# Transposing attention inputs by the DMA crossbar instead of TensorE, in a fused attention and feed-forward kernel

## The chip, the cores and the metric

One core of one Trainium2 chip. The metric is the device time of one execution in microseconds (us). The profiler's span, used for everything inside an execution, is 1.7 to 2.7 us shorter than that execution's time. The "granted clock" is the share of its full clock that TensorE was allowed, as the trace records it.

## The reference, cut to what matters

```python
# x: 8 batches, 8 heads, 512 tokens, 64 wide; state: 8, 8, 32, 64
a      = softmax(x @ state.T / 8);   xread = a  @ state     # tokens read the state
a2     = softmax(state @ x.T / 8);   sread = a2 @ x         # the state reads the tokens
y      = concat(xread, sread)        # 544 rows of 512 per batch
h      = y @ w_in                    # 512 -> 2048
g      = h + sin(alpha * h)**2 / (alpha + 1e-9)
out    = g @ w_out                   # 2048 -> 512
```

Two transposed operands are wanted per batch: x, to form the scores, and the softmax weights, to use them as a moving operand.

## The kernel before: the parts that matter

The kernel works in nine blocks t of 16 steps f. Block t makes g for batch t (block 8 does the state reads of all batches), and prepares the attention of batch t + 1 between its steps.

```python
def pack(a, g, parts=2):             # VectorE: x from head-major to token-major order ("repack")
    nc.vector.tensor_copy(a.xp[:, :, hs, :], xnat_l[a.b][:, hs, :].rearrange("p h (i d) -> p i h d", i=C))

def T(a, g):                         # 8 TensorE transposes of x, then a copy out of PSUM
    ...  nc.tensor.transpose(tp[:, k, i*P:(i+1)*P], a.pair(i, 2*g + k), ident[:])
    nc.vector.tensor_copy(a.xT[:, 2*g:2*g+2, :], tp[:])

def AT_(a, gs):  ...                 # the same for the softmax weights

def mm1(t, f):                       # h: PSUM pool of four buffers
    hp = psH.tile(...); two matmuls
    nc.scalar.activation(s, hp, ACT.Sin, scale=alpha)
    nc.gpsimd.tensor_tensor(s2, s, s, ALU.mult)
def snake(t, f, ...):                # the combine; frees the h buffer; issued two steps later
    nc.vector.scalar_tensor_tensor(gT, s2, inva, hp, ALU.mult, ALU.add)

# slots of block t, n = batch t+1          (steps; post = after the step's other work)
#   T at 0, 1   scores S at 3, 4   Exp X post 4   W at 6, column sums Cs at 7
#   row sums Rs post 7, 8   normalise N post 8, 9   AT_ at 12   m_step at 9, 11, 13, 15
#   load of x(t+2) post 5,  repack of x(t+2) post 15
```

`Cs` ends in a 128x128 reciprocal and two products on VectorE. `m_step` multiplies state by a quarter ("slab") of w_in. In all traces here an engine runs its instructions in program order.

The softmax here doesn't subtract the row's maximum and nothing guards it: scores larger than these inputs give would overflow.

Of the kernel before, what the change touches and what calls it, by code (L numbers as in the profile page):

```python
# [12 lines left out]
BF16 = mybir.dt.bfloat16  # L13
FP32 = mybir.dt.float32
# [4 lines left out]
def kernel(  # L19
# [9 lines left out]
    nc = tc.nc  # L29
# [4 lines left out]
    C = S // P  # L34
# [11 lines left out]
    const = ctx.enter_context(tc.tile_pool(name="const", bufs=1))  # L46
    wpool = ctx.enter_context(tc.tile_pool(name="wpool", bufs=1))
    xpool = ctx.enter_context(tc.tile_pool(name="xpool", bufs=3))
    xppool = ctx.enter_context(tc.tile_pool(name="xppool", bufs=3))
    apool = ctx.enter_context(tc.tile_pool(name="apool", bufs=2))  # L50
    smallp = ctx.enter_context(tc.tile_pool(name="smallp", bufs=2))
    gpool = ctx.enter_context(tc.tile_pool(name="gpool", bufs=2))
    sinp = ctx.enter_context(tc.tile_pool(name="sinp", bufs=4))
    outp = ctx.enter_context(tc.tile_pool(name="outp", bufs=3))
# [29 lines left out]
    w_in_sb = wpool.tile([P, Q, DFF], BF16, name="w_in_sb")  # L84
    w_in_v = moe_w_in.rearrange("(q p) f -> p q f", p=P)
    for k in range(FS):
        nc.gpsimd.dma_start(
            w_in_sb[:, :, k * FW:(k + 1) * FW], w_in_v[:, :, k * FW:(k + 1) * FW]
        )
    load_x(1, 1)  # L90
    w_out_sb = wpool.tile([P, FT, DOUT], BF16, name="w_out_sb")
    w_out_v = moe_w_out.rearrange("(ft p) c -> p ft c", p=P)
    for k in range(4):
# [22 lines left out]

    def prep_state():
        st2 = const.tile([P, 16, 2, D], BF16, name="st2")
        nc.vector.tensor_copy(
            st2[:], st_nat[:].unsqueeze(2).to_broadcast([P, 16, 2, D])  # L120
        )
        for half in range(2):
            tp = psX.tile([P, 8, P], BF16, name="st_ps", tag="px")
            for k in range(8):
                nc.tensor.transpose(
                    tp[:, k, :],
                    st2[:, half * 8 + k].rearrange("p r d -> p (r d)"),
                    ident[:],
                )
            for r in range(2):  # L130
                rows = slice(r * D, (r + 1) * D)
                src = tp[rows].rearrange("d k (e r2 jh) -> d e r2 jh k", r2=2, jh=2)
                dst = stT[rows].rearrange(
                    "d bg (h2 r2 jh hf k) -> d (bg h2) r2 jh hf k", h2=2, r2=2, jh=2, hf=2
                )
                if r == 0:
                    nc.vector.tensor_copy(dst[:, :, r, :, half, :], src[:, :, r])
                else:
                    nc.scalar.copy(dst[:, :, r, :, half, :], src[:, :, r])


    class Att:
# [2 lines left out]
            a.xp = xppool.tile([P, C, H, D], BF16, name="xp")  # L145

        def alloc(a):
            a.xT = apool.tile([P, Q, S], BF16, name="xT")
            a.E = apool.tile([P, G, C, P], BF16, name="E")
            a.A = apool.tile([P, G, C, P], BF16, name="A")  # L150
            a.AT = apool.tile([P, G, S], BF16, name="AT")
            a.R = smallp.tile([P, G, C * HH], FP32, name="R")
            a.rR = smallp.tile([P, G, C * HH], FP32, name="rR")
            a.sp = {}
# [11 lines left out]
        def T(a, g):  # L166
            tp = psX.tile([P, 2, S], BF16, name="x_ps", tag="px")
            for k in range(2):
                for i in range(C):
                    nc.tensor.transpose(  # L170
                        tp[:, k, i * P:(i + 1) * P], a.pair(i, 2 * g + k), ident[:]
                    )
            nc.vector.tensor_copy(a.xT[:, 2 * g:2 * g + 2, :], tp[:])  # L173

        def S(a, g):
            sp = psX.tile([P, C, P], FP32, name="s_ps", tag="px")
            for i in range(C):
                for k in range(2):
                    cols = slice(k * 2 * Ns, (k + 1) * 2 * Ns)
                    nc.tensor.matmul(  # L180
                        sp[:, i, cols],
                        a.xT[:, 2 * g + k, i * P:(i + 1) * P],
                        stT[:, a.b * G + g, cols],
                        start=True, stop=True,
                    )
            a.sp[g] = sp
# [68 lines left out]
    def m_step(b, fs, on_act):  # L255
        if fs == 0:
            Ms[b] = apool.tile([P, G, DFF], BF16, name="M")
        mp = [psX.tile([P, FW], FP32, name="m_ps", tag="px") for _ in range(G)]
        for h in range(2):
            for g in range(G):  # L260
                for r in range(2):
# [40 lines left out]
            gT[t][:, f, :n], s2[:, :n], inva_sb[:, f:f + 1], hp[:, :n], ALU.mult, ALU.add  # L302
        )

    def mm2(t, st, f0, f1, box):
        if f0 == 0:
            box[0] = psO.tile([P, DOUT], FP32, name="o_ps")
        op = box[0]
        for ft in range(f0, f1):
            nc.tensor.matmul(  # L310
                op[:], gT[t][:, ft, st * P:(st + 1) * P], w_out_sb[:, ft, :],
# [2 lines left out]
        if f1 == FT:  # L314
            o_sb = outp.tile([P, DOUT], FP32, name="o_sb")
            nc.scalar.copy(o_sb[:], op[:])  # L316
            if t < B:
                r0 = t * TB + st
                nc.sync.dma_start(out[r0:r0 + C * (P - 1) + 1:C, :], o_sb[:])
            else:  # L320
                for k in range(P // Ns):
                    r0 = (st * (P // Ns) + k) * TB + S
                    nc.sync.dma_start(out[r0:r0 + Ns, :], o_sb[k * Ns:(k + 1) * Ns, :])

    atts, Ms, gT = {}, {}, {}


    warm_up(12)
# [17 lines left out]
        m_step(0, k, (True, True))  # L346
    a.AT_([0])
    a.AT_([1])
    for k in range(2, 4):
        m_step(0, k, (True, True))  # L350
    atts[1] = Att(1)
    atts[1].pack(0, 1)

    LAG = 2
    pend = []
    box = [None]
    for t in range(B + 1):
        gT[t] = gpool.tile([P, FT, S], BF16, name="gT")
        pe, post = {}, {}

        def add(d, s, fn, *args):
            d.setdefault(s, []).append((fn, args))

        if t + 1 < B:
            n = atts[t + 1]
            n.alloc()
            add(pe, 0, n.T, 0)
            add(pe, 1, n.T, 1)
            add(pe, 3, n.S, 0)
            add(pe, 4, n.S, 1)  # L370
            add(post, 4, n.X, 0)
            add(post, 4, n.X, 1)
            add(post, 7, n.Rs, 0)
            add(post, 8, n.N, 0, nc.gpsimd)
            add(post, 8, n.Rs, 1)
            add(post, 9, n.N, 1, nc.gpsimd)
            add(pe, 12, n.AT_, [0, 1])
            for k, s in enumerate((9, 11, 13, 15)):
                add(pe, s, m_step, t + 1, k, (True, t == 0))
        if t < B:  # L380
            s = 6 if t + 1 < B else 0
            add(pe, s, atts[t].W)
            add(pe, s + 1, atts[t].Cs)
        if t + 2 < B:
            def nxt(b=t + 2):
                atts[b] = Att(b)
                atts[b].pack(0, 1)
            add(post, 5, load_x, t + 2, 1)
            add(post, 15, nxt)
        for f in range(FT):  # L390
            cur = mm1(t, f)
            for fn, args in pe.get(f, []):
# [1 line left out]
            pend.append((t, f) + cur)  # L394
            if len(pend) > LAG:
                snake(*pend.pop(0))
            if t > 0:
                mm2(t - 1, f // 4, (f % 4) * 4, (f % 4) * 4 + 4, box)
            for fn, args in post.get(f, []):
                fn(*args)  # L400
    while pend:
        snake(*pend.pop(0))
    for st in range(B * Ns // P):
        for k in range(4):
            mm2(B, st, 4 * k, 4 * k + 4, box)
# [1 line left out]
_INS = ['x', 'state', 'moe_w_in', 'moe_w_out', 'moe_alpha']  # L407
_OUTS = [((4352, 512), 'float32')]
# [25 lines left out]
```

## Time and profile before

| | before |
|---|---|
| time, median (the profiled execution: 265.33) | 266.09 us |
| first Sin of block 0 | 21.18 us |
| block 0, first Sin to first Sin | 24.46 us |
| block 1 | 26.93 us |
| blocks 2 to 6 | 27.27, 27.26, 27.26, 27.26, 27.12 us |
| block 7 | 22.02 us |
| first Sin of block 8 to the end | 32.77 us |

The seams between blocks are taken at the Sin of step 0. Each block switches ScalarE to Exp and back, and for 3.4 us GpSimd gets no new Sin: the Exp gap. A timeline gives start, length, engine; in brackets the idle time ahead and what ended it.

```profile
107.78 1.28 ACT L189 ACT_TABLE_LOAD   x1
112.06 0.96 DVE L243 RECIPROCAL rC<-w_ps 128x128 f32<-128x128 f32 x1 [2.39 <-PE w_ps L236]
112.24 1.04 POOL L297 TENSOR_TENSOR s<-s 128x512 bf16<-128x512 bf16 x1 [3.36 <-ACT s L295]
113.67 0.75 DVE L301 SCALAR_TENSOR_TENSOR gT<-s,inva_sb,h_ps 128x512 bf16<-128x512 bf16 x1
114.47 0.59 PE L284 MATMUL h_ps<-AT,M 128*128 128x512 bf16 x2 [0.21 <-DVE gT L301]
```

The reader is to see the order: VectorE starts the reciprocal at 112.06, before GpSimd has its first square after the gap, so most of that work lies in time that VectorE would have idled away. TensorE then waits only 0.21 us for an h buffer.

### The profile page before, as it was taken

The numbers are of one execution on the slowest core, as the hardware profiler recorded it, in microseconds if no ns is written. First come the engines' busy times: TensorE is split into PE (matmuls) and PEld (weight loads), VectorE is DVE, ScalarE is ACT, GpSimd is POOL, SyncE is SP. The second block draws the span as 40 slices with busy tenths as digits, with TensorE's granted clock in tenths as the row PEclk, the third lists the DMA queues.
The fourth block names the chain that finished last, engine by engine and source line by source line (L and its number), as shares of the span: only waits on it lengthen the run. The fifth ranks groups of instructions, "written<-read, shape, count | busy, mean of one in ns | idle before, by whom it ended". The sixth has DMA issues, their size and how long they took to land.

```text
span 263.5 us, 4423 instructions
## 1 busy us (share of the span) xinstructions
PE 231.6 (88%) x1630; PEld 110.2 (42%) x1660; DVE 164.2 (62%) x267; ACT 160.0 (61%) x254; POOL 171.8 (65%) x183
## 2 busy tenths in 40 slices
PE   6667557998989898989899989998999999999991
PEld 2424213543455344534453445434444444456640
DVE  3733667749774978397758866687668685543310
ACT  2454968495649664966487557865685655644420
POOL 8713599749844985499548955696659668854400
PEclk9856968999999999999999999999999999999997
DMA  7999860018111711172115411361111111111112
GB/s 84 201 201 205 148 80 4 1 41 120 42 42 40 115 47 40 40 110 53 40 42 82 78 44 41 56 105 40 42 41 40 42 40 40 42 55 64 44 62 59
DMA packets 19782, 17.86 MB, mean 68 GB/s; under 512 B 2992, under 2 KB 15280, under 8 KB 19760
## 3 DMA queue, kind: packets, MB, share of 16 engines
q0 software_dynamic: 12704, 8.65, 23.4%
q1 hardware_dynamic: 7056, 8.92, 10.3%
q8 instruction: 13, 0.21, 0.3%
q14 instruction: 9, 0.07, 0.1%
HBM read 17.31 MB, written 8.91 MB: 100 GB/s over the span
## 4 chain that ended last, share of the span: by engine, by line
PE 63%; DVE 21%; DMA 5%; POOL 4%; issue 3%; ACT 1%; ACTq 0%; POOLq 0%
PE o_ps L310 35%; PE h_ps L284 15%; DVE gT L301 8%; DMA xnat<-in_x_dram 5%; PE x_ps L170 3%; DVE R L193 3%; DVE rC L243 3%; PE h_ps L290 3%; DVE M L276 3%; PE m_ps L265 2%; POOL s L297 2%; DVE xp L158 2%; DVE xs_all L246 2%; PE w_ps L225 2%; DVE rR L194 1%
## 5 line engine op out<-in xcount | busy, mean ns | idle before, releaser
L297 POOL TENSOR_TENSOR s<-s 128x512 bf16<-128x512 bf16 (+1 forms) x144 | 141.7, 995 | 77.0 <-ACT s L295 76.8
L295 ACT ACTIVATE s<-h_ps,alpha_sb 128x512 bf16<-128x512 f32 (+1 forms) x144 | 94.0, 666 | 75.8 <-PE h_ps L284 63.7
L310 PE MATMUL o_ps<-w_out_sb,gT 128*128 128x512 bf16 x523 | 135.7, 380 | 2.0 <-issue 1.0
L301 DVE SCALAR_TENSOR_TENSOR gT<-s,inva_sb,h_ps 128x512 bf16<-128x512 bf16 (+1 forms) x144 | 99.9, 712 | 34.1 <-POOL s L297 33.9
L284 PE MATMUL h_ps<-AT,M 128*128 128x512 bf16 x247 | 76.5, 390 | 9.7 <-DVE gT L301 9.3
L310 PEld LDWEIGHTS <-gT 128*128 128x128 bf16 x544 | 48.6, 98 | 50.9 <-issue 5.5
L284 PEld LDWEIGHTS <-M 128*128 128x128 bf16 x256 | 24.9, 99 | 41.4 <-issue 15.9
L316 ACT COPY o_sb<-o_ps 128x512 f32<-128x512 f32 x34 | 20.0, 588 | 10.7 <-PE o_ps L310 9.2
L274 ACT CAST M<-m_ps 128x512 bf16<-128x512 f32 x40 | 22.4, 583 | 3.2 <-PE m_ps L265 3.2
L276 DVE CAST M<-m_ps 128x512 bf16<-128x512 f32 x24 | 16.2, 676 | 10.8 <-PE m_ps L265 10.8
L243 DVE RECIPROCAL rC<-w_ps 128x128 f32<-128x128 f32 x8 | 7.7, 957 | 17.0 <-PE w_ps L236 17.0
L265 PE MATMUL m_ps<-w_in_sb,stT 64*32 64x512 bf16 x256 | 16.3, 422 | 2.2 <-ACT M L274 2.0
L170 PE MATMUL x_ps<-ident,xp 128*128 128x128 bf16 x128 | 10.5, 231 | 7.5 <-DVE xp L158 7.5
L173 DVE COPY xT<-x_ps 128x1024 bf16<-128x1024 bf16 x16 | 11.0, 691 | 9.2 <-PE x_ps L170 9.2
L170 PEld LDWEIGHTS <-xp 128*128 128x128 bf16 x128 | 8.5, 104 | 13.5 <-DVE xp L158 11.5
L265 PEld LDWEIGHTS <-stT 64*32 64x32 bf16 x256 | 4.3, 90 | 17.6 <-issue 15.1
L193 DVE TENSOR_REDUCE R<-E 128x16 f32<-128x512 bf16 x16 | 10.8, 676 | 0.5 <-ACT E L189 0.5
L189 ACT ACTIVATE E<-s_ps 128x512 bf16<-128x512 f32 x16 | 8.8, 595 | 1.8 <-PE s_ps L180 1.6
L290 PE MATMUL h_ps<-xs_all,w_in_sb 128*128 128x256 bf16 x64 | 9.6, 273 | 0.1
L219 DVE COPY AT<-a_ps 128x1024 bf16<-128x1024 bf16 (+1 forms) x9 | 5.7, 632 | 6.1 <-PE a_ps L216 6.0
L189 ACT ACT_TABLE_LOAD x7 | 9.0, 1283 | 0.1
L295 ACT ACT_TABLE_LOAD x7 | 9.0, 1283 | 0.1
(41 smaller groups left out, 107.5 us busy)
## 6 DMA issues: line engine op xcount, KB each, us to landing
out_dram<-o_sb SPq DMA_DIRECT2D x32, 256.0 KB, 2.2
xnat<-in_x_dram POOLq DMA_DIRECT2D x7, 512.0 KB, 8.2
w_in_sb<-in_moe_w_in_dram POOLq DMA_DIRECT2D x4, 512.0 KB, 9.9
w_out_sb<-in_moe_w_out_dram POOLq DMA_DIRECT2D x4, 512.0 KB, 19.5
xnat<-in_x_dram POOLq DMA_DIRECT2D x2, 256.0 KB, 5.7
out_dram<-o_sb SPq DMA_DIRECT2D x8, 64.0 KB, 1.7
st_nat<-in_state_dram POOLq DMA_DIRECT2D x1, 256.0 KB, 4.8
alpha_sb<-in_moe_alpha_dram SPq DMA_DIRECT2D x1, 8.0 KB, 3.0
```

The lines of the kernel that those rows point to most:

```text
L170: nc.tensor.transpose(tp[:, k, i * P:(i + 1) * P], a.pair(i, 2 * g + k), ident[:])
L189: nc.scalar.activation(a.E[:, g], a.sp[g][:], ACT.Exp, scale=scale)
L193: nc.vector.reduce_sum(a.R[:, g], E8, axis=AX.X)
L265: nc.tensor.matmul(mp[g][o0:o0 + Ns, :], stT[rows, b * G + g, c0:c0 + Ns], w_in_sb[rows, 2 * g + h, fs * FW:(fs + 1) * FW], start=True, st ...
L274: nc.scalar.copy(dst, mp[g][:])
L276: nc.vector.tensor_copy(dst, mp[g][:])
L284: nc.tensor.matmul(hp[:, :n], Ms[t][:, g, f * P:(f + 1) * P], atts[t].AT[:, g, :], start=(g == 0), stop=(g == G - 1),)
L295: nc.scalar.activation(s[:, :n], hp[:, :n], ACT.Sin, scale=alpha_sb[:, f:f + 1])
L297: nc.gpsimd.tensor_tensor(s2[:, :n], s[:, :n], s[:, :n], ALU.mult)
L301: nc.vector.scalar_tensor_tensor(gT[t][:, f, :n], s2[:, :n], inva_sb[:, f:f + 1], hp[:, :n], ALU.mult, ALU.add)
L310: nc.tensor.matmul(op[:], gT[t][:, ft, st * P:(st + 1) * P], w_out_sb[:, ft, :], start=(ft == 0), stop=(ft == FT - 1),)
L316: nc.scalar.copy(o_sb[:], op[:])
```

## The change

Its intent: take 24 transposes per batch, and the copies out of PSUM, off TensorE and VectorE for batches 1 to 7; start block 0 as soon as half of w_in is there; spread block 0's output matmuls over blocks 0 and 1; shorten the end. The core of the diff (smaller edits at the head, which engine evicts what above all, are left out):

```diff
     for k in range(FS):
+        if k == 2:
+            load_x(1, 1)
         nc.gpsimd.dma_start(w_in_sb[...k], w_in_v[...k])
-    load_x(1, 1)
...
+        def T_dma(a):
+            nc.sync.dma_start_transpose(a.xT..., a.xp...)
+        def AT_dma(a):
+            nc.sync.dma_start_transpose(a.AT..., a.A...)
...
+        if t == 0:    # block 0: batch 1 packed and transposed after step 0, w_in slabs 2, 3 at steps 4, 6
+            add(post, 0, att, 1, "T_dma")
+            ss, xs, rs, tr = (2, 3), 3, 8, 11;   ps = (14, 15);   ms = steps 8, 10, 12, 14
+        else:
+            ss, xs, rs, tr = (1, 2), 2, 5, 8;    ps = (12, 13)
+            ws = [(5, 6, t)] ...                # W and Cs;  W and Cs of batch 0 in block 1
+        # S at ss, X post xs, Rs post rs, rs+1, N one later, AT_dma post tr
+        # load of x(t+2) post 3, repack post ps[0], ps[1], T_dma post ps[1]
...
+        if t == 0:  two[f] = two tiles of block 0's output matmuls, 2 + 2 per step, from step 9 on
...                  # the rest of them in block 1; later blocks as before
+            # last stores: one DMA per row tile, by a 3-d view
+            ov = out.rearrange("(b t) c -> b t c", t=TB)
+            eng.dma_start(ov[st * n:(st + 1) * n, S:, cols], o_sb[:, cols])
+    # and the last tile in two halves of 256 columns, evicted by ScalarE and VectorE
```

The pools for xp, the attention tiles and the small tiles get one more buffer.

More of the change, by code (lines that the diff above doesn't have):

```diff
@@ L48 @@
     xpool = ctx.enter_context(tc.tile_pool(name="xpool", bufs=3))
-    xppool = ctx.enter_context(tc.tile_pool(name="xppool", bufs=3))
-    apool = ctx.enter_context(tc.tile_pool(name="apool", bufs=2))
-    smallp = ctx.enter_context(tc.tile_pool(name="smallp", bufs=2))
+    xppool = ctx.enter_context(tc.tile_pool(name="xppool", bufs=4))
+    apool = ctx.enter_context(tc.tile_pool(name="apool", bufs=3))
+    epool = ctx.enter_context(tc.tile_pool(name="epool", bufs=3))
+    smallp = ctx.enter_context(tc.tile_pool(name="smallp", bufs=3))
     gpool = ctx.enter_context(tc.tile_pool(name="gpool", bufs=2))
@@ L118, in prep_state @@
         st2 = const.tile([P, 16, 2, D], BF16, name="st2")
-        nc.vector.tensor_copy(
-            st2[:], st_nat[:].unsqueeze(2).to_broadcast([P, 16, 2, D])
-        )
+        for half in range(2):
+            js = slice(half * 8, (half + 1) * 8)
+            nc.vector.tensor_copy(
+                st2[:, js], st_nat[:, js].unsqueeze(2).to_broadcast([P, 8, 2, D])
+            )
         for half in range(2):
@@ L135, in prep_state @@
                 )
-                if r == 0:
-                    nc.vector.tensor_copy(dst[:, :, r, :, half, :], src[:, :, r])
-                else:
-                    nc.scalar.copy(dst[:, :, r, :, half, :], src[:, :, r])
+                nc.scalar.copy(dst[:, :, r, :, half, :], src[:, :, r])
     class Att:
@@ L147, in alloc @@
         def alloc(a):
-            a.xT = apool.tile([P, Q, S], BF16, name="xT")
-            a.E = apool.tile([P, G, C, P], BF16, name="E")
+            a.xT = apool.tile([P, C, Q, P], BF16, name="xT")
+            a.E = epool.tile([P, G, C, P], BF16, name="E")
             a.A = apool.tile([P, G, C, P], BF16, name="A")
@@ L172, in T @@
                     )
-            nc.vector.tensor_copy(a.xT[:, 2 * g:2 * g + 2, :], tp[:])
+            nc.vector.tensor_copy(
+                a.xT[:, :, 2 * g:2 * g + 2, :],
+                tp[:].rearrange("p k (i t) -> p i k t", i=C),
+            )
+        def T_dma(a):
+            nc.sync.dma_start_transpose(
+                a.xT[:].rearrange("p i q t -> p (i q) t"),
+                a.xp[:].rearrange("p i h d -> p (i h d)"),
+            )
+        def AT_dma(a):
+            nc.sync.dma_start_transpose(
+                a.AT[:].rearrange("p g (i t) -> p (g i) t", i=C),
+                a.A[:].rearrange("p g i c -> p (g i c)"),
+            )
         def S(a, g):
@@ L181, in S @@
                         sp[:, i, cols],
-                        a.xT[:, 2 * g + k, i * P:(i + 1) * P],
+                        a.xT[:, i, 2 * g + k, :],
                         stT[:, a.b * G + g, cols],
@@ L257, in m_step @@
             Ms[b] = apool.tile([P, G, DFF], BF16, name="M")
-        mp = [psX.tile([P, FW], FP32, name="m_ps", tag="px") for _ in range(G)]
+        if b == 0 and fs < 2:
+            mp = [psH.tile([P, FW], FP32, name="h_ps") for _ in range(G)]
+        else:
+            mp = [psX.tile([P, FW], FP32, name="m_ps", tag="px") for _ in range(G)]
         for h in range(2):
@@ L303, in snake, with mm2 @@
         )
-    def mm2(t, st, f0, f1, box):
+    def mm2(t, st, f0, f1):
         if f0 == 0:
-            box[0] = psO.tile([P, DOUT], FP32, name="o_ps")
-        op = box[0]
+            ops[t, st] = psO.tile([P, DOUT], FP32, name="o_ps")
+        op = ops[t, st]
         for ft in range(f0, f1):
@@ L316, in mm2, with store, mm2_last @@
             nc.scalar.copy(o_sb[:], op[:])
-            if t < B:
-                r0 = t * TB + st
-                nc.sync.dma_start(out[r0:r0 + C * (P - 1) + 1:C, :], o_sb[:])
-            else:
-                for k in range(P // Ns):
-                    r0 = (st * (P // Ns) + k) * TB + S
-                    nc.sync.dma_start(out[r0:r0 + Ns, :], o_sb[k * Ns:(k + 1) * Ns, :])
-    atts, Ms, gT = {}, {}, {}
+            store(t, st, o_sb, slice(0, DOUT), nc.sync)
+    def store(t, st, o_sb, cols, eng):
+        if t < B:
+            r0 = t * TB + st
+            eng.dma_start(out[r0:r0 + C * (P - 1) + 1:C, cols], o_sb[:, cols])
+        else:
+            n = P // Ns
+            ov = out.rearrange("(b t) c -> b t c", t=TB)
+            eng.dma_start(ov[st * n:(st + 1) * n, S:, cols], o_sb[:, cols])
+    def mm2_last(t, st):
+        o_sb = outp.tile([P, DOUT], FP32, name="o_sb")
+        for k in range(2):
+            op = psO.tile([P, DOUT], FP32, name="o_ps")
+            cols = slice(k * DOUT // 2, (k + 1) * DOUT // 2)
+            for ft in range(FT):
+                nc.tensor.matmul(
+                    op[:, cols], gT[t][:, ft, st * P:(st + 1) * P], w_out_sb[:, ft, cols],
+                    start=(ft == 0), stop=(ft == FT - 1),
+                )
+            if k == 0:
+                nc.scalar.copy(o_sb[:, cols], op[:, cols])
+                store(t, st, o_sb, cols, nc.sync)
+            else:
+                nc.vector.tensor_copy(o_sb[:, cols], op[:, cols])
+                store(t, st, o_sb, cols, nc.scalar)
+    atts, Ms, gT, ops = {}, {}, {}, {}
     warm_up(12)
@@ L348, with plan @@
     a.AT_([1])
-    for k in range(2, 4):
-        m_step(0, k, (True, True))
-    atts[1] = Att(1)
-    atts[1].pack(0, 1)
-    LAG = 2
-    pend = []
-    box = [None]
-    for t in range(B + 1):
-        gT[t] = gpool.tile([P, FT, S], BF16, name="gT")
+    def plan(t):
         pe, post = {}, {}
@@ L362, in add @@
             d.setdefault(s, []).append((fn, args))
-        if t + 1 < B:
-            n = atts[t + 1]
-            n.alloc()
-            add(pe, 0, n.T, 0)
-            add(pe, 1, n.T, 1)
-            add(pe, 3, n.S, 0)
-            add(pe, 4, n.S, 1)
-            add(post, 4, n.X, 0)
-            add(post, 4, n.X, 1)
-            add(post, 7, n.Rs, 0)
-            add(post, 8, n.N, 0, nc.gpsimd)
-            add(post, 8, n.Rs, 1)
-            add(post, 9, n.N, 1, nc.gpsimd)
-            add(pe, 12, n.AT_, [0, 1])
-            for k, s in enumerate((9, 11, 13, 15)):
-                add(pe, s, m_step, t + 1, k, (True, t == 0))
@@ L380, with nxt, att @@
-        if t < B:
-            s = 6 if t + 1 < B else 0
-            add(pe, s, atts[t].W)
-            add(pe, s + 1, atts[t].Cs)
-        if t + 2 < B:
-            def nxt(b=t + 2):
-                atts[b] = Att(b)
-                atts[b].pack(0, 1)
-            add(post, 5, load_x, t + 2, 1)
-            add(post, 15, nxt)
+        def nxt(b, k):
+            if k == 0:
+                atts[b] = Att(b)
+            atts[b].pack(k)
+        def att(b, m, *args):
+            getattr(atts[b], m)(*args)
@@ new lines, in plan @@
+        n = t + 1
+        if t == 0:
+            for k in range(2):
+                add(post, 0, nxt, 1, k)
+            add(post, 0, att, 1, "alloc")
+            add(post, 0, att, 1, "T_dma")
+            add(pe, 4, m_step, 0, 2, (True, False))
+            add(pe, 6, m_step, 0, 3, (True, False))
+            ss, xs, rs, tr = (2, 3), 3, 8, 11
+            ms, ws = ((8, True, True), (10, True, False), (12, True, False), (14, True, False)), []
+            ps = (14, 15)
+        else:
+            ss, xs, rs, tr = (1, 2), 2, 5, 8
+            ms = ((8, True, False), (10, True, False), (12, True, False), (14, True, False))
+            ws = [(5, 6, t)] if n < B else [(0, 1, t)][:B - t]
+            if t == 1:
+                ws.append((11, 11, 0))
+            ps = (12, 13)
@@ new lines, in plan @@
+        if n < B:
+            for g in range(G):
+                add(pe, ss[g], att, n, "S", g)
+                add(post, xs, att, n, "X", g)
+                add(post, rs + g, att, n, "Rs", g)
+                add(post, rs + 1 + g, att, n, "N", g, nc.gpsimd)
+            add(post, tr, att, n, "AT_dma")
+            for k, (s, *on) in enumerate(ms):
+                add(pe, s, m_step, n, k, on)
+        for s0, s1, b in ws:
+            add(pe, s0, att, b, "W")
+            add(pe, s1, att, b, "Cs")
@@ new lines, in plan @@
+        if t + 2 < B:
+            add(post, 3, load_x, t + 2, 1)
+            for k in range(2):
+                add(post, ps[k], nxt, t + 2, k)
+            add(post, ps[1], att, t + 2, "alloc")
+            add(post, ps[1], att, t + 2, "T_dma")
+        two = {}
+        if t == 0:
+            for f in range(9, FT):
+                two[f] = [(0, st, 2 * (f - 9), 2 * (f - 8)) for st in range(2)]
+        elif t == 1:
+            two[1] = [(0, 0, 14, 16), (0, 1, 14, 16)]
+            for f in range(2, FT):
+                k0, k1 = 32 * (f - 2) // 14, 32 * (f - 1) // 14
+                for h in range(2):
+                    a0, a1 = max(k0, 16 * h), min(k1, 16 * h + 16)
+                    if a0 < a1:
+                        two.setdefault(f, []).append((0, 2 + h, a0 - 16 * h, a1 - 16 * h))
+        else:
+            for f in range(FT):
+                two[f] = [(t - 1, f // 4, (f % 4) * 4, (f % 4) * 4 + 4)]
@@ L390 @@
+        return pe, two, post
+    LAG = 2
+    pend = []
+    for t in range(B + 1):
+        gT[t] = gpool.tile([P, FT, S], BF16, name="gT")
+        pe, two, post = plan(t)
         for f in range(FT):
@@ L396 @@
                 snake(*pend.pop(0))
-            if t > 0:
-                mm2(t - 1, f // 4, (f % 4) * 4, (f % 4) * 4 + 4, box)
+            for args in two.get(f, []):
+                mm2(*args)
             for fn, args in post.get(f, []):
@@ L402 @@
         snake(*pend.pop(0))
-    for st in range(B * Ns // P):
-        for k in range(4):
-            mm2(B, st, 4 * k, 4 * k + 4, box)
+    n = B * Ns // P
+    for st in range(n - 1):
+        mm2(B, st, 0, FT)
+    mm2_last(B, n - 1)
 _INS = ['x', 'state', 'moe_w_in', 'moe_w_out', 'moe_alpha']
```

## The prediction

> **What bounds the kernel now.** I read the page's busy rows first, then busy time in stretches, then TensorE's waits, then the timeline of one block. The program runs nine blocks, t = 0 to 8, of 16 steps. A step is two matmuls into h_ps (L284), Sin on ScalarE, a square on GpSimd, a combine on VectorE (L301), and four output matmuls (L310) for the block before. The attention of the next block is slotted in between steps.
>
> ```profile
> PE   6667557998989898989899989998999999999991
> POOL 8713599749844985499548955696659668854400
> PEclk9856968999999999999999999999999999999997
> DMA  7999860018111711172115411361111111111112
> ```
>
> A digit is a fortieth of 263.5 us, 6.6 us. From slice 8 on PE is nearly full; in the first seven it is half empty, at a reduced clock, while DMA is nearly full. In stretches (length, then PE, PEld, DVE, ACT, POOL busy, clock, DMA share, GB/s):
>
> ```profile
> 16.30:46.00 29.70, 19.83 (x152) 8.79 (x154) 17.50 (x28) 20.34 (x34) 18.91 (x19) 0.74 0.78 120
> 100.50:127.70 27.20, 25.50 (x188) 11.88 (x192) 19.49 (x31) 18.13 (x29) 19.23 (x19) 1.00 0.28 59
> ```
>
> A middle block is bound by TensorE: 25.50 of 27.20 us, no other engine over 19.5. Block 0 is bound by no engine; it is a chain. TensorE's waits over four middle blocks (us in total, times, longest), then the timeline (start, length, engine):
>
> ```profile
> PE x_ps L170 <- DVE xp L158: 3.8, 5, 0.8
> PE h_ps L284 <- DVE gT L301: 2.7, 8, 0.5
> ```
>
> ```profile
> 20.50 0.63 PE L284 MATMUL h_ps<-AT,M 128*128 128x512 bf16 x1 [0.33 <-issue]
> 21.60 0.69 DVE L158 COPY xp<-xnat 128x2048 bf16<-128x2048 bf16 x1 [3.89 <-DMA xnat<-in_x_dram]
> ...
> 99.69 0.75 DVE L158 COPY xp<-xnat 128x2048 bf16<-128x2048 bf16 x1
> 100.50 0.62 PE L170 MATMUL x_ps<-ident,xp 128*128 128x128 bf16 x8 [0.77 <-DVE xp L158]
> 100.96 1.03 PE L310 MATMUL o_ps<-w_out_sb,gT 128*128 128x512 bf16 x4
> ...
> 120.31 0.61 PE L216 MATMUL a_ps<-ident,A 128*128 128x128 bf16 x8
> 120.76 1.03 PE L310 MATMUL o_ps<-w_out_sb,gT 128*128 128x512 bf16 x4
> ```
>
> Starts count here, not lengths, because matmuls overlap: eight transposes hold the array from 100.50 to 100.96, 0.46 us, though their record says 0.62. Once per block PE also stands idle 0.77 us until VectorE has repacked x (L158). At the head, block 0's first h_ps matmul comes at 20.50, after all four slabs of w_in; PE then waits for x of batch 1, which lands at 21.60 as the last of that queue.
>
> **What the Trainium skill says.** "VectorE: DVE Perf Modes", section "The three transpose paths", gives 390 ns on TensorE and 1309 ns by the crossbar for one 128x128 bf16 transpose. Here TensorE's record is 219 ns and the array is held only 0.46 us / 8 = 58 ns, so what is bought on PE is small per piece; the crossbar must be judged by latency, not by work saved. "DMA: Bandwidth & Descriptors", section "Latency and other measured facts", gives an effective 261 GB/s for a transposing DMA whose middle dim is not contiguous, and the section on the anatomy of a DMA a fixed cost near 2.0 us. The trace has no transposing DMA; for plain stores its landings agree with a fixed part of that size:
>
> ```profile
> out_dram<-o_sb SPq DMA_DIRECT2D x32, 256.0 KB, 2.2
> out_dram<-o_sb SPq DMA_DIRECT2D x8, 64.0 KB, 1.7
> ```
>
> The same page, section "Issuing engines are not separate DMA queues", says that all queues share the 16 engines. The DMA row bears on that: 9, 9, 9, 8 in the slices in which the first transpose would run.
>
> **The change, part by part.** Block lengths before, from successive first matmuls of a block: block 0 from 20.5 to about 45.4, blocks 1 to 5 27.26 us each (L170 after L158 at 73.23, 100.50, 127.76, 155.03, 182.29), block 6 about 26.6, block 7 about 21.8, block 8 20.8 (16 steps of six full matmuls' worth at 0.216 us), tail 12.6, to 263.5.
>
> *Removed from TensorE*, per batch 1 to 7: 16 x-transposes, 2 x 0.46 = 0.91 us; 8 weight transposes, 0.45 us; the wait for the repack, 0.77 us. Sum 2.13 us, on the path wherever PE is the bound. *Removed from VectorE*: two copies of 0.69 and one of 0.69 us, 2.07 us. VectorE is not the bound, but the combines come through sooner; of 2.7 us / 4 = 0.65 us per block of PE waiting for them I take off 0.3. A middle block without new waits: 27.26 - 2.13 - 0.3 = 24.8 us.
>
> *Added*: two crossbar transfers per batch, 512 KB (x) and 256 KB (weights). Estimate from the skill's figures: 512 KB / 261 GB/s = 2.0, plus 2.0 fixed, 4.0 us. I choose L = 4.5 us for x, since issuing many small tiles should cost something; the weights 3.5.
>
> *Is L hidden?* In the middle blocks the repack's second half now stands after step 13. Before, the repack placed after step 15 ran 2.3 us after that step's first matmul (97.40 to 99.69). So the transfer starts at about 2.3 + 0.41 + 0.1 = 2.8 us after step 13's start. The scores that read it stand behind step 1 of the next block: four steps of 1.55 us and two matmuls later, 6.6 us. Slack is 3.8 us; with L = 4.5, PE waits 0.7 us. Middle block: 25.5 us, 1.75 less. The weights' transfer stands after step 8 and is needed eight steps (12 us) later, with about 4 us of GpSimd lag ahead of it: hidden.
>
> *Head*: block 0 needs two slabs. The second landed by 13.83; eight matmuls, eight transposes and two copies of 0.43 us follow, and the four tiles no longer wait in the two-buffer pool. First h_ps matmul at about 16.3, 4.2 us sooner. But x of batch 1 lands third, near 16.4, is packed by 17.3, and then its transpose shares the engines with w_in and w_out: I take 6.5 us, landing at 23.8. The scores block PE after step 2, so step 3 starts near 24.0 against 25.3 before: most of the 4.2 us is given back.
>
> *Block 0 and 1*: 28 of block 0's 64 output matmuls (28 x 0.216 = 6.0 us) move from block 1 into block 0, where PE has room. Block 0 is then paced by GpSimd: 13 remaining squares at 1.04, two normalisations at 1.04, one load issue of 0.95, and an Exp gap (two table loads of 1.28 and two Exp of 0.6, partly buffered): 19 us, so it ends near 43. Block 1 has 18 us of PE work, so GpSimd paces it too: 19.7 us, about 1 of Exp gap, and, as transposes are issued late in block 0 (weights after step 11, x after step 15), about 2.6 us of new waits: 23.3 us. Block 2 starts at 66.3 against 72.6.
>
> *Tail*: the last tile's eviction is halved (0.59 to about 0.35 us) and the last four stores become two. "DMA: Bandwidth & Descriptors", section on why a DMA raises its semaphore by 16, says a transfer runs on the largest number up to 16 that divides both slowest dims; the destination's slowest dim is now 4, so 4 engines. I take 0.7 us off: 11.9.
>
> *Sum*: 66.3 + 5 x 25.5 + 21.8 + 20.8 + 11.9 = 248.3 us of span; time is 266.09 - 263.5 = 2.6 above span: 250.9, rounded to 250.
>
> **Rivals.** (1) *The transposes turn into a wait.* The page gives no crossbar duration, and every us of L beyond 3.8 falls on each of five middle blocks, plus about two at the head: some 7 us per us of L. L of 6 gives 260, 7 gives 267, 8 gives 274. For it: 1309 ns for 32 KB in the skill is a poor rate, and PE executes in order, so one late landing stops everything. Against: the late slots look chosen with a known latency. (2) *All is hidden*, L under 3.8: middle blocks 24.8 or less, block 1 near 21, about 243. (3) *Another engine becomes the bound.* GpSimd needs 19.2 us per middle block, ScalarE 18.1, VectorE 19.5 - 2.1: none reaches 24.8, so only blocks 0 and 1 change their bound. (4) *The gain is in the head and nothing else counts*: then 260; but 2.13 us per middle block is real PE occupancy, so I give this little.
>
> **Range and chances.** L between 3 and 6 gives 240 to 260; a slower first transpose adds a few us: 239 to 264 holds 8 in 10. Faster by over 2% means below 260.8, so L below about 6.1: 0.77. Within 2%, L of 6 to 7.6: 0.14. Slower: 0.09.
>
> **What would show it.** Middle blocks of 25 to 26 us between first matmuls; no L170 or weight transposes on PE after batch 0; a PE wait of under 1.5 us per block in front of the scores; the transposing DMA landing in 4 to 5 us in the middle and 6 to 7 at the head; first h_ps matmul near 16; blocks 0 and 1 with GpSimd busier than PE. The prediction is wrong if a transpose takes 7 us or more, if stores and transposes on the SyncE queue hold each other up, or if block 0 and 1 keep their old length.

## The result, and the profile after

The time went up: 285.56 us median (283.74 to 286.51) against 266.0 in the same rounds, a ratio of 1.073 with a 95% interval of 1.066 to 1.080. Ratios are the mean time of one kernel's fast runs over that of the other's of the same rounds, so not quite the ratio of the medians. From the page of the changed kernel, and from its list of DMAs:

```profile
PE   8450079957588898987999798979898999999990
PEclk9975555897979999999999999999999999999997
DMA  7999932123260427325460735072412011111111
xT<-xp SPq DMA_TRANSPOSE x7, 4.3
AT<-A SPq DMA_TRANSPOSE x7, 3.0
```

A slice is now 7.1 us. In slices 3 and 4, counted from 0 (21 to 36 us), PE reads 0: next to nothing runs there. The last two lines give the median time from issue to landing, 4.3 us for x and 3.0 for the weights, so the latency that the prediction turned on came out as estimated. Busy time in stretches (block 0, block 1, a middle block), to be held against the prediction's two lines:

```profile
17.00:61.00 44.00, 23.31 (x125) 7.65 (x124) 16.55 (x28) 17.42 (x27) 19.39 (x19) 0.65 0.62 97
61.00:93.00 32.00, 23.22 (x165) 9.41 (x164) 19.11 (x33) 18.46 (x28) 19.28 (x19) 0.89 0.38 71
120.23:147.08 26.85, 24.32 (x170) 10.54 (x169) 17.79 (x30) 18.27 (x29) 19.37 (x20) 1.00 0.46 95
```

What TensorE waited for from 93 to 227 us, in blocks 2 to 6 (us, times, longest):

```profile
PE h_ps L303 <- DVE gT L320: 8.2, 5, 1.6
PE s_ps L196 <- DMA xT<-xp: 4.0, 4, 1.2
```

The first line is a wait for a combine to free an h buffer, the second for a crossbar transpose to land. In the whole run they are 13.8 and 25.4 us. The timeline at the first and at the second crossbar transpose:

```profile
17.42 7.59 SPq L180 DMA_TRANSPOSE xT<-xp  x1
35.37 0.61 PE L196 MATMUL s_ps<-stT,xT 128*128 128x64 bf16 x8 [17.47 <-DMA xT<-xp]
...
60.80 1.79 SPq L180 DMA_TRANSPOSE xT<-xp  x1
65.42 0.61 PE L196 MATMUL s_ps<-stT,xT 128*128 128x64 bf16 x8 [3.99 <-DMA xT<-xp]
```

The first transpose holds PE until 35.37, 17.95 us after its issue; the second takes 4.6 us. The same instruction issues for 7.59 us in one place and 1.79 in the other. Where the 20.1 us of longer span went, block by block (differences of Sin starts, worked out from the traces):

| stretch | before | after | difference |
|---|---|---|---|
| to the first Sin | 21.18 | 16.74 | -4.4 |
| block 0 | 24.46 | 44.35 | +19.9 |
| block 1 | 26.93 | 31.96 | +5.0 |
| blocks 2 to 6, sum | 136.17 | 133.91 | -2.3 |
| block 7 | 22.02 | 22.02 | 0 |
| block 8 and tail | 32.77 | 34.64 | +1.9 |

Four questions follow: why the first transpose is slow, why the middle blocks gain so little, why block 1 is long, and why the tail is longer. The Exp gap of the changed kernel shows a candidate for the second:

```profile
103.50 0.75 DVE L320 SCALAR_TENSOR_TENSOR gT<-s,inva_sb,h_ps 128x512 bf16<-128x512 bf16 x1 [3.65 <-POOL s L316]
105.05 0.90 DVE L259 RECIPROCAL rC<-w_ps 128x128 f32<-128x128 f32 x1
107.40 0.59 PE L303 MATMUL h_ps<-AT,M 128*128 128x512 bf16 x2 [1.65 <-DVE gT L320]
```

Here VectorE idles 3.65 us until the square comes, then does a combine, and only then the reciprocal that before had run inside the gap. TensorE pays 1.65 us.

### The profile page after: what moved, and what is told of

It reads as the page before. It is cut to its first block, busy times and chain, and to the rows that moved or that the text cites. A ratio compares the mean times of both kernels' runs of the same rounds, so it can differ in the third digit from the quotient of the medians.

```text
span 283.6 us, 4170 instructions
## 1 busy us (share of the span) xinstructions
PE 228.8 (81%) x1508; PEld 102.6 (36%) x1508; DVE 155.7 (55%) x258; ACT 159.6 (56%) x251; POOL 172.0 (61%) x183
## 4 chain that ended last, share of the span: by engine, by line
PE 34%; POOL 21%; issue 16%; DMA 13%; DVE 10%; ACT 3%; POOLq 0%; ACTq 0%
PE o_ps L329 18%; POOL s L316 17%; DMA xT<-xp 9%; PE h_ps L303 8%; DVE gT L320 4%; DMA w_in_sb<-in_moe_w_in_dram 3%; PE m_ps L284 2%; PE h_ps L309 2%; DVE rC L259 2%; ACT s L314 1%; PE o_ps L354 1%; DVE M L295 1%; POOL A L220 1%; DVE xp L159 1%; POOL A L217 1%
## 5 line engine op out<-in xcount | busy, mean ns | idle before, releaser
L329 PE MATMUL o_ps<-w_out_sb,gT 128*128 128x512 bf16 x528 | 139.1, 386 | 0.8 <-DVE gT L320 0.7
L303 PE MATMUL h_ps<-AT,M 128*128 128x512 bf16 x256 | 81.1, 402 | 13.9 <-DVE gT L320 13.8
L303 PEld LDWEIGHTS <-M 128*128 128x128 bf16 x256 | 25.4, 101 | 49.0 <-issue 23.6
L295 DVE CAST M<-m_ps 128x512 bf16<-128x512 f32 x29 | 20.0, 688 | 37.7 <-PE m_ps L284 37.7
L196 PE MATMUL s_ps<-stT,xT 128*128 128x64 bf16 x128 | 7.1, 203 | 26.1 <-DMA xT<-xp 25.4
L293 ACT CAST M<-m_ps 128x512 bf16<-128x512 f32 x31 | 17.8, 578 | 0.4 <-PE m_ps L284 0.4
L196 PEld LDWEIGHTS <-xT 128*128 128x128 bf16 x128 | 5.9, 105 | 31.9 <-DMA xT<-xp 29.0
L284 PE MATMUL m_ps<-w_in_sb,stT 64*32 64x512 bf16 x240 | 14.3, 423 | 1.8 <-ACT E L205 1.4
L159 DVE COPY xp<-xnat 128x1024 bf16<-128x1024 bf16 x16 | 10.4, 655 | 2.2 <-DMA xnat<-in_x_dram 2.2
L217 POOL TENSOR_TENSOR A<-E,rR 128x512 bf16<-128x512 bf16 x8 | 8.3, 1042 | 0.0
```

The source lines that it names most:

```text
L284: nc.tensor.matmul(mp[g][o0:o0 + Ns, :], stT[rows, b * G + g, c0:c0 + Ns], w_in_sb[rows, 2 * g + h, fs * FW:(fs + 1) * FW], start=True, st ...
L293: nc.scalar.copy(dst, mp[g][:])
L295: nc.vector.tensor_copy(dst, mp[g][:])
L303: nc.tensor.matmul(hp[:, :n], Ms[t][:, g, f * P:(f + 1) * P], atts[t].AT[:, g, :], start=(g == 0), stop=(g == G - 1),)
L329: nc.tensor.matmul(op[:], gT[t][:, ft, st * P:(st + 1) * P], w_out_sb[:, ft, :], start=(ft == 0), stop=(ft == FT - 1),)
```

## The experiments

Each is one edit of the changed kernel unless it says otherwise; all gave correct results. In two of the four sets of runs the kernel before itself ranged from 265.5 to 271.2 us; eight of those fourteen runs are slow by the records (over 1.5% above the fastest), and ratios use the fast ones alone. The sets ran on different chips. Differences of under 2% are therefore read from the traces and not from ratios.

### No load beside the first transpose

```diff
-    (w_in slabs 2, 3 and w_out requested at the start)
+    for k in range(2, FS): add(post, 3, load_w_in, k)      # in block 0
+    for k in range(4):     add(post, 3, load_w_out, k)
```

> The changed kernel, with the last two slabs of w_in and all of w_out requested only after step 3 of block 0, so that nothing else is in flight while the first crossbar transpose runs. Contention theory: the transpose moves 2048 packets of 256 B (128 per DMA engine) and waits for one load packet (about 94 ns) per own packet while loads are queued; alone it should land 4.3 to 4.6 us after its issue instead of 17.9, its issue should last 1.8 us instead of 7.6, and PE should resume near 22 us instead of 35.4. The loads then come late, so block 0 still waits for w_in: block 0 between 29 and 37 us instead of 44.4, total 271 to 279 us. Rival, the first transpose of a program is slow whatever runs beside it: it still takes 15 us or more and the total rises above 290 us.

Measured: 274.53 us. The first transpose in this trace:

```profile
17.67 2.47 SPq L182 DMA_TRANSPOSE xT<-xp  x1
22.12 0.61 PE L198 MATMUL s_ps<-stT,xT 128*128 128x64 bf16 x8 [3.81 <-DMA xT<-xp]
```

PE resumes 4.45 us after the issue instead of 17.95, and block 0 takes 35.25 us, most of the rest now a wait for the late slabs (6.0 us at once for w_in). So the first transpose is not slow by being first; it is slow beside the loads. Three other runs that left both as they were show the long wait again, 17.1 to 17.7 us. The DMA records of the changed kernel say how. The transpose consists of 2048 packets of 256 B. Between 25.0 and 35.3 us the trace holds 1502 of them and 1444 load packets of 1 KB: about one for one. A record does not name its engine, so the order on each engine is inferred from the counts. A load packet takes 96 ns, an own packet 30.5. If each of the 16 engines takes one of either kind in turn, its 2048 / 16 = 128 own packets need, as an estimate, 128 x (96 + 30.5) ns = 16.2 us; from the first packet to the last, completion included, it was 13.6, since packets overlap somewhat, and the first packet came 4.0 us after the issue. In bytes the transpose got a fifth of the traffic, not half.

### Batch 1 transposed on TensorE

```diff
-            add(post, 0, att, 1, "T_dma")
+            for g in range(G): add(pe, 1, att, 1, "T", g)
```

> The changed kernel, with the x of batch 1 alone transposed on TensorE as before (the other six on the crossbar). If the one late landing in block 0 is the largest loss: block 0 (first Sin to first Sin) falls from 44.4 to 22 to 25 us, the rest stays as in the changed kernel (block 1 near 32, middle blocks 26 to 27), total 264 to 267 us. Rival, block 0 is slow for its extra output matmuls and the w_in matmuls moved into it: block 0 stays above 30 us and the total above 272 us.

Measured: 266.97 us; block 0 took 24.89 us, block 1 30.00, blocks 2 to 5 26.88 to 27.78. So nearly the whole excess of block 0 was the one landing; the extra output matmuls cost next to nothing there. 17.5 us of it are the wait itself. After the wait TensorE also ran at a lower granted clock (0.69 from 35.4 to 61 us in the changed kernel, 0.95 in this run's block 0), which may be the other 2 us; that is not tested. Without this landing the change as a whole is level with the kernel before (ratio 0.998, 0.985 to 1.011). That is not yet the worth of the other six crossbar batches, since the new order of steps and the tail are in it too; the runs with split stores and without the crossbar, below, take these apart.

### Repack and transpose four steps earlier

```diff
-            ps = (14, 15)      # block 0
+            ps = (10, 11)
-            ps = (12, 13)
+            ps = (8, 9)
```

> The changed kernel, with repack and crossbar transpose of the x of batches 2 to 7 issued four steps earlier. Theory A, the landing wait (1.2 us per middle block, 4.0 in block 1) also causes the waits for the combines behind it (about 2 us per block), because it comes just ahead of the Exp gap and leaves GpSimd dry twice: both go, middle blocks fall from 26.8 to 24.5 to 25.2 us, block 1 from 32 to 27 to 29, total 285.6 to about 273. Theory B, the waits for the combines come from the bunched reductions on VectorE alone: only the landing wait goes, middle blocks 25.5 to 26, total about 277 to 280.

Measured: 287.58 us, no faster, and neither theory holds. The landing waits after the first were gone, and block 1 fell to 27.05 (4.9 us for a landing wait of 4.0), but middle blocks grew to 28.3 and 29.6: waits for the combines from 93 to 227 us rose from 8.2 us to 16.4. The timeline of this run shows a cause that I had not thought of, on VectorE, and below it on GpSimd and TensorE:

```profile
132.22 3.71 DVE L159 COPY xp<-xnat 128x1024 bf16<-128x1024 bf16 x1
135.84 0.74 DVE L320 SCALAR_TENSOR_TENSOR gT<-s,inva_sb,h_ps 128x512 bf16<-128x512 bf16 x1
136.50 0.41 DVE L159 COPY xp<-xnat 128x1024 bf16<-128x1024 bf16 x1
```

```profile
132.61 3.02 POOL L316 TENSOR_TENSOR s<-s 128x512 bf16<-128x512 bf16 x3
136.63 0.59 PE L303 MATMUL h_ps<-AT,M 128*128 128x512 bf16 x2 [2.05 <-DVE gT L320]
```

The first half of the repack takes 3.71 us, the second, of the same shape, 0.41. The long one begins while GpSimd is at work and ends 0.3 us after GpSimd's run of three squares ends (132.61 + 3.02 = 135.63). Combines, which read PSUM, run beside squares without this (0.65 to 0.75 us with or without a square). The Trainium skill, "SBUF — State Buffer", section "SBUF: two separate sides", says that VectorE, in some fast modes, and GpSimd take turns on one exclusively locked port pair. The traces fit that. Over all of them but the one of the slow execution below, 101 repacks of this shape begin while a GpSimd product is at work, and 100 of them end 0.28 to 0.37 us after the end of one, whenever that is; with GpSimd idle 60 of 69 took 0.41 to 0.43. In 91 cases the copy waited for one product alone; in nine, five of this run and four of the later one with the repack at 11 and 12, through three or four in a row. What decides between the two is open. The theory now: the repack is cheap only where GpSimd pauses or is about to, and the changed slots met that in part, by luck (0.48 and 1.16 us in the middle of its trace).

### Last stores split by batch again

```diff
-            ov = out.rearrange("(b t) c -> b t c", t=TB)
-            eng.dma_start(ov[st * n:(st + 1) * n, S:, cols], o_sb[:, cols])
+            for k in range(P // Ns):
+                r0 = (st * (P // Ns) + k) * TB + S
+                eng.dma_start(out[r0:r0 + Ns, cols], o_sb[k * Ns:(k + 1) * Ns, cols])
```

> The changed kernel, with the last stores split by batch again (32 partitions each) while the halved last eviction stays. Theory: the merged stores run on 4 DMA engines because their destination's slowest dim is 4, and three of them queue up behind each other at the end; split, the time from the first Sin of block 8 to the end falls from 34.6 to 31.5 to 32.8 us and the total by 2 to 3 us. Rival, the tail is long for the halved matmuls: no change (within 0.5 us).

Measured: 282.99 us; from the first Sin of block 8 to the end 31.86 us instead of 34.64, and 32.77 before. So the rest of the change in the tail, such as the halved last tile, is worth 0.9 us, and the merged stores cost 2.8. The trace of the changed kernel has 4.0 to 4.4 store packets in flight at a time from 276 to 281 us, where this run reaches 9.4, and the last store's first packet at 279.83 us although VectorE's eviction ended at 276.65: it queued up behind the others.

### The new order without the crossbar

```diff
-            add(post, 0, att, 1, "T_dma");  add(post, ps[1], att, t + 2, "T_dma");  add(post, tr, att, n, "AT_dma")
+            T(0), T(1) on TensorE at steps 14, 15 (of block 1 for batch 2 at step 0, of batch 1 at step 1)
+            add(pe, 13 if t == 0 else 11, att, n, "AT_", [0, 1])
```

> The changed kernel with every transpose back on TensorE and its new order of steps kept. It separates the crossbar from the new order. If the crossbar is worth its landing waits in the middle (1.36 us of PE work saved against 1.0 us of waiting per block), middle blocks get 0.3 to 1.2 us longer than the 26.8 of the changed kernel, block 0 is 23 to 26 us, total 264 to 271. If the new order of steps is what costs (waits for the combines of about 1.65 us per block, which the kernel before did not have), these waits stay here though no crossbar runs; if they are caused by the crossbar they vanish and middle blocks come near 26.5.

Measured: 271.24 us, ratio 1.021 to before; block 0 24.68 us, middle blocks 28.16. Two things follow. The combine waits are there without any crossbar: 6.6 us in the four blocks from 100 to 211, 1.6 us the longest. So they belong to the new order of steps. And this order costs 0.9 us per middle block against before; the crossbar, waits and all, took 1.4 of 28.16 off again on average over blocks 2 to 5 (1.0 to 2.1), a little more than I had expected. In these slots the transposes also bring a wait of their own: 2.9 us from 100 to 211 us for a PSUM buffer in front of the x-transposes.

### Column sums one step earlier

```diff
-            ws = [(5, 6, t)] if n < B else ...
+            ws = [(4, 5, t)] if n < B else ...
```

> The changed kernel, with the state-read matmuls and their column sums (and so the 128x128 reciprocal and two products on VectorE) one step earlier, at steps 4 and 5. Theory: in the changed order they stand behind the combine of step 3, which waits for the Exp gap to end, so 1.5 us of VectorE work that ran inside the gap before now runs after it and PE waits 1.65 us for an h_ps buffer. One step earlier they are ahead of that combine and run in the gap: this wait falls below 0.5 us, middle blocks from 26.8 to 25.2 to 25.8, total 285.6 to 276 to 280. Rival, the wait comes from the landing wait ahead of the gap: no change in the combine wait, middle blocks stay above 26.4.

Measured: 278.47 us. Blocks 2 to 5 took 26.04, 25.76, 25.98, 25.77 us. TensorE's waits from 90 to 219 us in this run:

```profile
PE s_ps L196 <- DMA xT<-xp: 5.1, 5, 1.2
PE h_ps L303 <- DVE gT L320: 1.0, 5, 0.2
```

The combine waits fell from 1.65 to 0.2 us each by moving one group of instructions ahead of one combine in VectorE's order. The landing wait stayed, so it had not caused them: the rival is out.

### Three mends together, and the repack moved by one step

The three mends are batch 1 on TensorE, split last stores and earlier column sums. In the second run the repack also moves from steps 12, 13 to 11, 12 (12, 13 in block 0).

> Changed kernel with three mends only: x of batch 1 on TensorE, last stores on 16 engines, column sums one step earlier; the repack stays where the change put it, at steps 12 and 13. If the repack at steps 11 and 12 lost 0.5 us or more per block to a busy GpSimd (one half took 2.58 us there), middle blocks are 25.6 to 26.0 here against 26.3 to 27.0 there, and the total is 251 to 254, 1 to 4 us below it, though the landing wait (near 1.2 us per block) is back. If the stretched half cost nothing on the path, this run is slower, 256 or more.

> Changed kernel with four mends: x of batch 1 on TensorE, last stores on 16 engines, column sums one step earlier, repack and crossbar transpose of x one step earlier. Block 0 near 24.9, block 1 27 to 28.5, middle blocks 24.5 to 25.5, total 250 to 258. If the repack one step earlier runs into a busy GpSimd (as the one four steps earlier did, 3.71 us instead of 0.41), middle blocks stay near 26 and the total near 259.

Measured: 259.15 us (ratio 0.974, 0.970 to 0.978) and 254.90 us (0.958, 0.953 to 0.963). The first is a miss in total: I had overlooked that block 1 stays at 29.83 us there, with its landing wait of 4.0, against 26.75. Block 0 was longer too, 26.02 against 24.75 us, at a granted clock of 0.83 against 0.93 from 16.2 to 41 us; why is not tested. The second came out as expected in total, but its middle blocks are those of its rival. The middle of the first is as expected but for one block: 25.8 to 26.05 us in three of four blocks (one of 27.56) without the move, 26.27 to 27.0 with it, although the move takes the landing waits away: over blocks 2 to 6 the two are level (130.8 and 130.6 us). The second run's VectorE and GpSimd show the price:

```profile
113.77 2.58 DVE L159 COPY xp<-xnat 128x1024 bf16<-128x1024 bf16 x1
...
117.53 0.41 DVE L159 COPY xp<-xnat 128x1024 bf16<-128x1024 bf16 x1
```

```profile
112.04 4.02 POOL L316 TENSOR_TENSOR s<-s 128x512 bf16<-128x512 bf16 x4
```

The squares end at 116.06, the long half of the repack at 116.35. Block 6, which has no repack of a later batch, took 24.51 us in the same run. That is about what a block without these waits costs.

### The repack inside the Exp gap

x loaded one block earlier, repack at step 5 behind the column sums, and the three mends.

```diff
+                for k in range(2): add(pe, 5, nxt, t + 2, k)       # repack; then alloc and T_dma
+            if t + 3 < B: add(post, 11, load_x, t + 3, 1)
```

> As the combination before, but x is loaded a block ahead and repacked inside the Exp gap (step 5), where GpSimd has nothing to do; the crossbar transpose then has ten steps to land. If a busy GpSimd stretches the repack, it takes 0.41 us per half here, no landing wait is left and middle blocks are 24.2 to 24.9, total 247 to 254. If the repack is slow for another reason it stays at 0.7 us or more per half and delays the combine behind it: middle blocks 25.5 or more.

Measured: 260.38 us, a miss: middle blocks 26.67 to 28.10. The gap was already taken. The reciprocal waits for the column sums until 105.36 us, and the repack starts at 106.96, after GpSimd's first square at 105.54. Its two halves took 2.15 us, and the four squares beside it 4.46 instead of 4.02: each slows the other. Here each half waited for one square and then held up the next.

### The repack on ScalarE

```diff
+            copy = nc.vector.tensor_copy if a.b < 2 else nc.scalar.copy
-            nc.vector.tensor_copy(a.xp..., xnat...)
+            copy(a.xp..., xnat...)
```

With the three mends, once at steps 9 and 11, once as the only edit of the run with the repack at 11 and 12:

> As the three mends, but the repacks of batches 2 to 7 run on ScalarE, halves at steps 9 and 11, so that they cannot meet GpSimd on VectorE and the transpose is issued two steps earlier. Theory, both the landing wait and the collision of repack and GpSimd are what separates middle blocks (25.8) from block 6 (24.5, no repack and no wait): landing wait 0, combine waits below 1 us per block, middle blocks 24.4 to 25.2, total 246 to 251. Rival, ScalarE becomes the pace: its copies take over 1 us each and Sin comes late, middle blocks 25.5 or more, total 252 or more.

> The combination with the repack at steps 11 and 12, with one thing changed: the repacks of batches 2 to 7 go to ScalarE. If a VectorE copy stretched by a busy GpSimd made the middle blocks 26.3 to 27.0 there, they fall to 24.6 to 25.2 and the total from 254.9 to 246 to 249. If the slots were the reason (and the run with ScalarE repacks gained from its earlier ones), they stay above 25.8 and the total above 251.

Measured: 246.13 us (ratio 0.925, 0.922 to 0.928) and 247.67 us. The first run's middle block and its repacks (count, then shortest, median and longest in ns):

```profile
92.17:116.81 24.64, 24.30 (x170) 10.61 (x169) 17.10 (x27) 19.84 (x31) 19.17 (x20) 1.00 0.46 97
L160 ACT COPY xp<-xnat x12: 1034/1046/1056, 35.4 to 160.0; 128x1024 bf16<-128x1024 bf16 x12
```

A half costs 1.05 us on ScalarE, 2.5 times VectorE's best (0.41), but never more than 1.07 in these two runs, busy GpSimd or not. Middle blocks are 24.64 us with PE busy for 24.30 of them, and PE's only wait from 67 to 190 us is 1.0 us for combines. The second run changes nothing but the engine of the repack against its parent: blocks 2 to 5 went from 26.27 to 27.0 us to 24.78, 24.93, 26.59 and 25.01, and 254.90 us to 247.67 (different chips; each ran beside the kernel before). So the copy on VectorE is what these blocks had paid for; that a busy GpSimd is what stretches it rests on the 100 of 101 copies above. The 26.59 is a block whose transpose landed after 5.92 us.

### The mended kernel without the crossbar

> The run with ScalarE repacks and the three mends, but every transpose on TensorE: what the crossbar itself is worth once its waits are gone. 1.36 us of PE work comes back per batch (16 x-transposes 0.91, 8 of the weights 0.45) plus VectorE copies of 2.07 us: middle blocks 24.64 + 1.4 to 2.2, so 26.0 to 26.8, total 253 to 259 against 246.1. If PE was not the bound in those blocks, they stay below 25.5 and the total below 251.

Measured: 261.1 us over three fast runs (ratio 0.971, 0.960 to 0.982), 15 us above the 246.1 of its twin with the crossbar (0.925), which ran in another set. I expected 7 to 13. Its profiled execution, a slow one, took 1187 us, with four 512-column matmuls in 5.29 us. That trace holds no clock record, so the 1.00 listed for it says nothing. No trace therefore shows where the extra 2 us or more come from, and this stays open; the wait for a PSUM buffer that the same slots brought in the earlier run is a candidate, and slots better fitted to TensorE transposes were not tried. The sign is clear: once its waits are off the path, the crossbar pays against these slots, and by more than its TensorE work.

## Why the prediction was wrong, point by point

I put the time at 250 us and it was 285.56; the measured span, 283.6, is 35.3 us above the predicted 248.3. **The step that failed** is in the head: "its transpose shares the engines with w_in and w_out: I take 6.5 us, landing at 23.8". It landed after 17.95 us, at 35.4. By "shares" I had added 2.0 us, as if the transpose kept half of the bandwidth; it got every other packet, with packets of a quarter of the size. "DMA: Bandwidth & Descriptors", section "Queues, rings and completion order", states that the engines alternate between queues packet by packet. I cited another section of that page and not this one; the trace agrees in the counts, 1502 to 1444. Block 0 came to 44.35 us against 26.7 in the sum, 17.7 of the 35.3. Rival (1), the transpose turned into a wait, named the right kind of loss in the wrong place: I spread it over the middle blocks by a latency that was in fact right.

**Block 1**, 31.96 us against 23.3: the landing wait and the combine waits, 2.6 us in the sum, were 4.0 and 4.4, and they cost more than their length, it seems because GpSimd paces this block: GpSimd ran dry 5.55 us behind the landing and 3.36 in the Exp gap just after. With the mends and the repack on ScalarE block 1 is 24.66.

**Middle blocks**, 26.8 us on average against 25.5, together 6.4 us. The landing wait, 0.7 in the sum, was 1.0 on average in the four blocks that have one, 1.2 at most: right in kind, small in error. The term of the sum that had the wrong sign is the "0.3" that I took off for combines coming sooner. They came later: 8.2 us in five blocks against 3.3 in the five before, since the change put the column sums' VectorE work behind a combine that waits out the Exp gap. I had counted how much work left VectorE and not looked at its order. The run with earlier column sums shows it: 1.0 us of these waits instead of 8.2.

**Tail**: 0.7 us off became 1.9 us on. I had the four engines from the skill and took only the last transfer, when three such transfers queue up.

**A slip in the sum**: the 2.6 us between time and span are the median of three runs less the span of another execution, which took 265.33 us. Its own gap is 1.8 us, which makes 250.1 and not 250.9; rounded it is the same.

**What held**: the first h matmul at 15.69 us (16.3), landings of 4.3 and 3.0 us (4.5 and 3.5), and the block without new waits, 24.8, which the mended runs show as 24.51 to 24.65. The crossbar's saving was real, 1.4 us per middle block against the same order without it; the change as scheduled gave it back at four places, and the largest was the first.

## What to carry to other kernels

Do not issue a transposing DMA with small packets beside bulk loads when an engine that works in order will wait for it: count the packets of both, not the bytes. When work is moved between steps, check for each in-order engine what now stands behind an instruction that waits. A copy that is cheap alone on VectorE may be better on a slower engine that GpSimd does not hold up, as ScalarE here.

## What the Trainium skill lacked or had wrong

- "DMA: Bandwidth & Descriptors" has no figure for a transposing DMA beside ordinary loads. Its rules table says that a transpose next to ordinary DMAs needs nothing, which is about correct results; the landing here went from 4.3 to 17.9 us, and the issue from 1.8 to 7.6.
- The same page has no landing time for a transpose from SBUF to SBUF. Here 512 KB landed in 4.3 us and 256 KB in 3.0; its 261 GB/s and 2.0 us (the latter from its section on a DMA issued by GpSimd) give an estimate of 4.0 and 3.0, which agrees. In three runs one x transpose took 5.9 us (5.93, 5.86, 5.92); in each a 16 KB packet of instructions, 0.93 to 0.96 us long, lay inside it, but others with such a packet beside them landed in 4.2 to 4.7 us. The cause is not tested.
- "VectorE: DVE Perf Modes", section "The three transpose paths", gives 1309 ns per 128x128 by the crossbar. As a rate it misleads: 16 of them in one DMA landed in 4.3 us, 0.27 us each.
- "SBUF — State Buffer" says that the later of the two waits for the other's whole instruction, and names slowdowns of 6.8 and 1.5 times without their shapes. The traces agree in 91 of 101 copies. Not in the page: nine copies of 128x1024 bf16 that waited through three or four GpSimd products in a row (0.41 to 3.71 us), and the cost to GpSimd, four squares in 4.46 instead of 4.02 us beside such copies.
- The rule of "DMA: Bandwidth & Descriptors" on how many engines a DMA uses, four here, is neither lacking nor wrong as far as the runs show: 4.0 to 4.4 packets in flight against up to 9.4, and a tail of 34.64 against 31.86 us.
- "TensorE: Matmul & The Clock Gate" has clock records that cannot be trusted and a clock gate stuck for 50 us and more. It has no whole execution of 1185 us without a clock record, in which a 512-column matmul took 1.3 us; it was seen once and excluded.
